# An attention and mixture-of-adapters kernel: products of zeros, the place of one pair's edges, and the piece size of k

## The chip, the cores and the metric

The kernel runs on one core of a Trainium2 chip. The metric is device time in microseconds of one launch: for the kernel before, the median of three runs is 186.81 us (186.53 to 188.19). One more execution was taken with the profiler; its rows are the source of every duration here.

Names of the engines in the rows: PE is TensorE (PEld its weight loads), DVE is VectorE, ACT is ScalarE, POOL is GpSimd, SP is SyncE, which here issues nearly all DMAs. SPq and ACTq are the DMA issues of those two engines.

## The reference

Attention for 8 batches, 8 heads, 576 tokens and head size 64, with a bias that depends on the distance of two tokens alone, and behind it an adapter layer for each token: the two best of 8 experts, each of rank 16.

```python
scores = scale * np.matmul(q, k.transpose(0, 1, 3, 2))
rel = pos[:, None] - pos[None, :]
n = np.abs(rel)                       # buckets of n, all n >= 128 in the last bucket
scores = scores + bias.transpose(2, 0, 1)[None, :, :, :]
attn = np.exp(scores - max); attn = attn / (attn.sum(-1) + 1e-09)
x = np.matmul(attn, v)                # then (B*S, H*D)
...
logits = x @ w_gate                   # top 2 of 8 experts, softmax over the two
delta[mask] += w[mask, k, None] * ((x[mask] @ A[e]) @ B[e])
return x + delta
```

## The kernel before

**Units.** Heads are taken two at a time: a unit u is a batch and a pair of heads, 32 units in all, four to a batch. The 576 tokens of a unit are split into 512 main tokens and the 64 last ones (the "tail"), whose loads and casts are done for a whole batch at a time.

**One unit.** q and k come from memory in float32 into staging tiles (four of each), are cast to bfloat16 (mostly by POOL), and are turned by PE: `turn` (L373) writes the transposes into a score tile in PSUM, and DVE copies them to SBUF. The same turn also takes other items: the tail of a batch (`tl_item`), and blocks of finished outputs on their way to the adapter layer (`x_item`, `zt_item`). Then `keys(u, c)` (L453), four times, forms the scores of 128 keys by 512 queries for both heads (L458), adds the banded part of the bias by products with the table (L463), and ACT takes the exp of the whole 128x1024 tile (L466). `edges(u)` (L507) forms the scores between main and last tokens (L515 and L518, exp in L520). `edge_l` on POOL and `edge_t` on DVE multiply the bias into the edges. `step(u, j)` (L655) multiplies by v and normalises on DVE (L583, L584).

**Score tiles.** Three PSUM tiles of 128x1024 float32 go round in a ring: each turn, each main tile and each edges takes the next one, and waits until the one that had it three places before has been read (by ACT's exp, or by DVE's copies for a turn). Two smaller PSUM tiles serve the products with v and everything else.

**Order.** All of the order is written out by hand: each engine does its instructions in the order in which the program names them, and waits where an input is missing. SP issues loads in program order too. The lines around the change come in this order: the first loads, memsets and the bias table; then products of zeros (`keep_busy`, L677, 128x512 each, whose result nobody reads); the turn of unit 0 together with the tail of two pairs; more zero products; the casts of unit 1's k; edges(0); the turn of unit 1; zero products; DVE's cast of the other tails; `near_first` (L202, one exp of a piece of the bias table Wt on ACT); edges(1); the main tiles of unit 0. Behind the start stands a loop over u from 2: in pass u the unit's main tiles are formed, unit u-1 is multiplied by v, and unit u+2 is turned. `next_edges` (L889) then forms the edges of unit u+1, right behind the transposes, or, where unit u+1 needs the batch tail that this very turn brings (`behind`, L893), after the second half of the step.

**Two ways to load k.** `load` (L102) puts four consecutive tokens of a head on one partition for q, and for k of the units below `WHOLE`: one DMA of 256 KB for the two heads, in pieces of 4 x 64 x 4 bytes = 1 KB. From `WHOLE` on k comes as v does: one DMA of 128 KB for each head, in which the pieces are single tokens, 256 bytes. In the first way the keys lie in another order on the partitions after the turn, so the copy out of the turn takes the four key blocks by themselves with a strided read (L398) and the rest in a second instruction (L400); in the second way one copy (L400) does all. `qk_item` (L411) chooses by naming its closure `keys_done` for the units below `WHOLE`, which `turn` looks at for `n0`.

Of the kernel before, what the change touches and what calls it, by code (L numbers as in the profile page):

```python
# [26 lines left out]
def _ap(t, offset, dims):  # L27

    return bass.AP(tensor=t.tensor, offset=t.offset + offset, ap=[list(t.ap[0])] + dims)
# [8 lines left out]
def kernel(  # L38
# [11 lines left out]
    nc = tc.nc  # L50
# [32 lines left out]
    def score_tile(name, shape=(128, 2, SM), dt=FP32):  # L83
        ring.append(ring.pop(0))
        return scps[ring[-1]].tile(list(shape), dt, name=name, tag="sc")
# [3 lines left out]
    NU = len(units)  # L89


    WHOLE = 4
    NV = 3
    PT = 64 + 2 * SM
    vts = [cp.tile([128, 4, 2, W1], BF16, name=f"v{i}", tag=f"v{i}") for i in range(NV)]
# [6 lines left out]
    def load(u, names="qkv", eng=nc.sync):  # L102
        b, hp = units[u]
        for nm in names:
            src = {"q": q, "k": k, "v": v}[nm]
            t = stg.tile([128, 2, 4 * D], FP32, name=f"{nm}s", tag=f"{nm}s")
            heads = src[b, 2 * hp:2 * hp + 2, :SM, :]
            if nm == "v" or (nm == "k" and u >= WHOLE):
                for h in range(2):
# [91 lines left out]
    def near_first():  # L201
        nc.scalar.activation(Wn[:, 0], Wt[:, 0, NB0:], ACT.Exp, scale=scale)  # L202
# [21 lines left out]
    def table_row(rows, hp, y):  # L224
        return Wn[rows, hp, y - NB0:y - NB0 + 64]

    def turned(h):
        return anti[h * 64:h * 64 + 64, 64 - 64 * h:128 - 64 * h]

    def factors_l(g0, g1):  # L230
        n = (g1 - g0) * 64
        ps = [mp.tile([128, 512], FP32, name="fl", tag="mm") for _ in range(2)]
        for hp in range(g0, g1):
            o = (hp - g0) * 64
            for x in range(2):
                for f in range(2):
                    for h in range(2):
                        nc.tensor.matmul(_ap(ps[h][f * 64:f * 64 + 64], o + x * 16, [[32, 2], [1, 16]]),
                                         lhsT=table_row(slice(h * 64, h * 64 + 64), hp, 256 - 64 * x),
                                         rhs=_ap(turned(h), 2 * f, [[1, 2], [4, 16]]),  # L240
                                         start=(hp == g0 and x == 0), stop=True, skip_group_check=True)
            for h in range(2):
                rows = slice(h * 64, h * 64 + 64)
                nc.tensor.matmul(ps[h][rows, n + o:n + o + 64], lhsT=turned(h),
                                 rhs=table_row(rows, hp, 128), start=False, stop=True, skip_group_check=True)
        for h in range(2):
            rows = slice(h * 64, h * 64 + 64)
            nc.vector.tensor_copy(EL[:, g0:g1, h, :], ps[h][:, :n].rearrange("p (g x) -> p g x", g=g1 - g0))
            nc.vector.tensor_copy(EC[rows, g0 * 64:g1 * 64], ps[h][rows, n:2 * n])
# [120 lines left out]
            t.group, t.k = g, k  # L370
        return g

    def turn(items, copy=nc.vector.tensor_copy, corner=None, after=None, first=None):  # L373
        n = sum(it[1] for it in items)
        n0 = 4 if items[0][0].__name__ == "keys_done" else 0
        assert n <= (16 if corner is None else 12)
        pf = score_tile("tx")
        ps = pf.rearrange("p a x -> p (a x)").bitcast(BF16).rearrange("p (a x) -> p a x", a=2)
        if corner is not None:
            cs = pf[:, :, 384:]  # L380
            corner_scores(corner, lambda hp: cs[:, hp // 2, (hp % 2) * 64:(hp % 2) * 64 + 64],
                          lambda hp: hp % 2 == 0)
        sb = txp.tile([128, 16, 2, 64], BF16, name="tx", tag="tx")
        s0 = 0
        for _, k, src, quarter in items:
            for i in range(k):
                c = s0 + i
                for a in range(2):
                    rows = slice(a * 64, a * 64 + 64)
                    cols = slice(c * 64, c * 64 + 64)  # L390
                    if quarter:
                        for h in range(2):
                            nc.tensor.transpose(ps[h * 64:h * 64 + 64, a, cols], src(i, a, h), ident[rows, rows])
                    else:
                        nc.tensor.transpose(ps[:, a, cols], src(i, a), ident[rows, rows])  # L395
            s0 += k
        if n0:
            (first or copy)(sb[:, :4].rearrange("p c a i -> p (c a i)").rearrange("p (a i c) -> p a i c", a=2, c=4),  # L398
                            ps[:, :, :256].rearrange("p a (c i) -> p a i c", c=4))
        copy(sb[:, n0:n], ps.rearrange("p a (c i) -> p c a i", i=64)[:, n0:n])  # L400
        if after is not None:
            after()
        if corner is not None:
            pxs[corner] = ep.tile([128, HP, 64], BF16, name="pcx", tag="pcx")
            nc.scalar.activation(pxs[corner].rearrange("p (a g) i -> p a (g i)", a=2), cs, ACT.Exp, scale=scale)  # L405
        s0 = 0
        for done, k, *_ in items:
            done(sb, s0)
            s0 += k

    def qk_item(u):  # L411
        n = [nat.pop((u, nm)) for nm in ("k", "q")]

        def done(sb, s0):
            qkT[u] = sb[:, s0:s0 + 8].rearrange("p (n c) a i -> p n (c a i)", n=2)

        def keys_done(sb, s0):
            done(sb, s0)
        return keys_done if u < WHOLE else done, 8, lambda i, a: n[i // 4][a * 64:a * 64 + 64, i % 4].rearrange("p h d -> p (h d)"), False

    def tl_item(b, g0=0, g1=HP):
        n = nat[(b, "qk")]

        def done(sb, s0):
            for hp in range(g0, g1):
                tl[(b, hp)] = sb[:, s0 + hp - g0].rearrange("p a i -> p (a i)")
        return (done, g1 - g0, lambda i, a: n[a * 64:a * 64 + 64, 2 * (g0 + i):2 * (g0 + i) + 2].rearrange(
            "p h d -> p (h d)"), False)
# [24 lines left out]
    def keys(u, c):  # L453
        b, hp = units[u]
        kT, qT = qkT[u][:, 0, :], qkT[u][:, 1, :]
        sc = score_tile("sc")
        for rows, prt, h, f in QUADS:
            nc.tensor.matmul(sc[prt, h, :],  # L458
                             lhsT=kT[rows, c * 128 + f * 64:c * 128 + f * 64 + 64],
                             rhs=qT[rows, :], start=True, stop=False, skip_group_check=True)  # L460
        for rows, prt, h, f in QUADS:
            p0, n, y0 = BAND[2 * c + f]
            nc.tensor.matmul(_ap(sc[prt, h, :], p0, [[128, 4], [1, n]]), lhsT=turned(h),  # L463
                             rhs=band(rows, u, y0, 0, 1, n),
                             start=False, stop=True, skip_group_check=True)
        nc.scalar.activation(probs[u][0][:, c, :, :], sc, ACT.Exp, scale=scale)  # L466
# [20 lines left out]
    def corner_scores(b, place, first):  # L487
        for hp in range(HP):
            t = tl[(b, hp)]
            for h in range(2):  # L490
                rows = slice(h * 64, h * 64 + 64)
                nc.tensor.matmul(place(hp)[rows], lhsT=t[rows, 64:], rhs=t[rows, :64], start=first(hp),
                                 stop=True, skip_group_check=True)
# [13 lines left out]
    def edges(u):  # L507
        b, hp = units[u]
        kT, qT = qkT[u][:, 0, :], qkT[u][:, 1, :]
        t = tl[(b, hp)]  # L510
        sc = score_tile("sc")
        for c in range(4):
            for h in range(2):
                rows = slice(h * 64, h * 64 + 64)
                nc.tensor.matmul(sc[:, h, c * 64:c * 64 + 64], lhsT=kT[rows, c * 128:c * 128 + 128],  # L515
                                 rhs=t[rows, :64], start=(c == 0), stop=True, skip_group_check=True)
        for rows, prt, h, f in QUADS:
            nc.tensor.matmul(sc[prt, h, 256:], lhsT=t[rows, 64:], rhs=qT[rows, f * 256:f * 256 + 256],  # L518
                             start=False, stop=True, skip_group_check=True)
        nc.scalar.activation(probs[u][1][:, 64:], sc.rearrange("p h x -> p (h x)"), ACT.Exp, scale=scale)  # L520
# [156 lines left out]
    def keep_busy(n):  # L677
        for _ in range(n):
            nc.tensor.matmul(busy, lhsT=zero[:, :128], rhs=zero, start=True, stop=True, skip_group_check=True)
# [22 lines left out]
    cast_tail(0, "qk", nc.vector, 0, 2)  # L702
    presets()
    cast(1, "q", nc.gpsimd)
    keep_busy(9)
    turn([qk_item(0), tl_item(0, 0, 2)])
    keep_busy(4)
    for h in range(2):
        cast_half(1, "k", h, nc.vector)
# [1 line left out]
        open_probs(u)  # L711
    edges(0)
    turn([qk_item(1)])
    keep_busy(3)
    cast_tail(0, "qk", nc.vector, 2)
    near_first()
    edges(1)
    keys(0, KO[0])
    cast(2, "q", nc.vector)
    cast(2, "k", nc.gpsimd)  # L720
    keys(0, KO[1])
    factors_l(0, 1)
    edge_l(0)
    keys(0, KO[2])
# [116 lines left out]
    for u in range(2, NU - 2):  # L841
# [40 lines left out]
        items = []  # L882
# [129 lines left out]
    s0 = ring[0]  # L1012
# [109 lines left out]
```

## Time and profile before

| | us |
|---|---|
| median of 3 runs | 186.81 |
| the profiled execution | 187.02 |
| its span, first to last instruction | 185.0 |
| PE busy in the span | 170.3 |
| ACT busy | 163.0 |
| DVE busy | 135.4 |
| POOL busy | 112.4 |

The profiled execution takes 2.0 us more than its span: that lies around the first and the last instruction. PE busy counts a matmul from its start to its modelled end. A row of a timeline gives start, time, engine, line, operation, result and operands, count, and in brackets how long the engine had been idle and what ended that. A row can stand for several instructions that ran together. In rows of DMA issues the time is that of the issue, not of the transfer.

### The profile page before, as it was taken

To read this page: it belongs to the slowest core of one execution; us is meant where nothing else is said; L and a number is where in the kernel's file an instruction comes from. 1 tells how busy PE (TensorE), PEld (TensorE's weight loads), DVE (VectorE), ACT (ScalarE), POOL (GpSimd) and SP (SyncE) were. 2 spreads that over 40 slices of the span, in tenths; PEclk is the share of its full clock that TensorE was granted. 3 is DMA by queue.
4 is the path that set the end of the run, shared out by engine and by line. 5 is a ranking of instruction groups with operands and counts; after the bars stand their busy time and mean duration, and the time that the engine had idled before them with its cause. 6 is when DMAs were issued, how large, how long until landed. Compare 5 with 4: busy or idle time off the path is not lost.

```text
span 185.0 us, 9915 instructions
## 1 busy us (share of the span) xinstructions
PE 170.3 (92%) x4254; PEld 123.4 (67%) x4276; DVE 135.4 (73%) x353; ACT 163.0 (88%) x199; POOL 112.4 (61%) x253
## 2 busy tenths in 40 slices
PE   7988898999998999999999999999999999999980
PEld 2346475776665777777777777777677677788950
DVE  6555875685855787778887798779778888788780
ACT  2189999999897999999999999999999989987880
POOL 8335679357649863985298538955495948435230
PEclk9999999999999999999999999999999999999999
DMA  4899798989889899999979987999988976333337
GB/s 141 214 247 265 179 217 186 235 193 228 212 218 225 200 250 274 233 240 253 244 189 233 262 230 212 227 235 253 246 226 220 267 193 174 121 117 114 117 145 255
DMA packets 93331, 39.26 MB, mean 212 GB/s; under 512 B 78816, under 2 KB 88552, under 8 KB 93288
## 3 DMA queue, kind: packets, MB, share of 16 engines
q1 hardware_dynamic: 92644, 38.16, 79.9%
q8 instruction: 33, 0.54, 1.3%
q10 hardware_dynamic: 644, 0.48, 1.3%
q14 instruction: 10, 0.08, 0.2%
HBM read 29.10 MB, written 9.44 MB: 208 GB/s over the span
## 4 chain that ended last, share of the span: by engine, by line
PE 58%; ACT 10%; DMA 7%; DVE 7%; SPq 5%; issue 5%; POOL 4%; POOLq 0%; DVEq 0%; ACTq 0%
PE pv L544 14%; PE sc L458 11%; ACT pk L466 8%; PE tx L395 6%; PE sc L463 4%; DMA qkt<-in_k_dram 4%; PE sc L515 3%; PE sc L518 3%; PE pv L591 3%; PE pv L561 3%; SPq L110 3%; PE pv L552 3%; DMA vs<-in_v_dram 2%; DMA qs<-in_q_dram 2%; DVE xn L584 2%
## 5 line engine op out<-in xcount | busy, mean ns | idle before, releaser
L466 ACT ACTIVATE pk<-sc 128x1024 bf16<-128x1024 f32 x120 | 113.1, 1032 | 5.1 <-PE sc L463 4.4
L458 PE MATMUL sc<-tx 64*64 64x512 bf16 x480 | 44.3, 389 | 1.8 <-ACT pk L466 0.8
L544 PE MATMUL pv<-v,pk 128*128 128x65 bf16 x992 | 41.3, 193 | 2.8 <-PE sc L463 1.9
L544 PEld LDWEIGHTS <-pk 128*128 128x128 bf16 x1024 | 37.6, 97 | 8.9 <-issue 2.3
L520 ACT ACTIVATE pt<-sc 128x1024 bf16<-128x1024 f32 x32 | 33.5, 1048 | 5.0 <-PE sc L518 4.4
L400 DVE COPY tx<-tx 128x2048 bf16<-128x2048 bf16 (+7 forms) x34 | 33.7, 991 | 2.9 <-PE tx L395 2.6
L463 PE MATMUL sc<-W,anti 64*64 64x192 bf16 (+1 forms) x464 | 34.3, 276 | 0.0
L584 DVE TENSOR_TENSOR xn<-pv,rc 128x320 bf16<-128x320 f32 x62 | 30.5, 491 | 2.1
L583 DVE RECIPROCAL rc<-pv 128x5 f32<-128x5 f32 x62 | 12.0, 193 | 20.6 <-PE pv L591 11.0
L140 POOL CAST kn<-ks 128x512 bf16<-128x512 f32 x30 | 18.7, 623 | 13.5 <-DMA ks<-in_k_dram 8.1
L458 PEld LDWEIGHTS <-tx 64*64 64x64 bf16 x480 | 15.6, 105 | 12.4 <-issue 2.3
L319 DVE TENSOR_TENSOR ot<-dl,xn 128x512 f32<-128x512 f32 x25 | 17.2, 688 | 7.4 <-PE sc L463 5.2
L136 POOL CAST v<-vs 128x512 bf16<-128x512 f32 x32 | 20.4, 636 | 3.3 <-PE pv L563 2.3
L525 POOL TENSOR_TENSOR pt<-pt,EL 128x128 bf16<-128x128 bf16 x32 | 13.7, 427 | 11.4 <-ACT pt L520 8.8
L504 POOL TENSOR_TENSOR pc<-pcx,EC 128x256 bf16<-128x256 bf16 (+2 forms) x9 | 5.6, 619 | 22.8 <-ACT pcx L405 14.2
L140 POOL CAST qn<-qs 128x512 bf16<-128x512 f32 x30 | 18.6, 621 | 0.8 <-DMA qs<-in_q_dram 0.8
L561 PE MATMUL pv<-v,pt 128*128 128x65 bf16 x248 | 17.9, 194 | 0.0
L552 PE MATMUL pv<-vb,pt 128*128 128x130 bf16 x124 | 17.4, 223 | 0.0
L463 PEld LDWEIGHTS <-anti 64*64 64x64 bf16 x480 | 15.1, 107 | 0.2
L561 PEld LDWEIGHTS <-pt 128*128 128x128 bf16 x256 | 14.1, 98 | 0.1
L395 PEld LDWEIGHTS <-kn 64*128 64x128 bf16 x256 | 5.9, 96 | 10.2 <-issue 5.9
L591 PE MATMUL pv<-AW,tx 128*128 128x136 bf16 x124 | 12.5, 224 | 0.0
(149 smaller groups left out, 285.9 us busy)
## 6 DMA issues: line engine op xcount, KB each, us to landing
qs<-in_q_dram SPq DMA_DIRECT2D x32, 256.0 KB, 4.1
vs<-in_v_dram SPq DMA_DIRECT2D x64, 128.0 KB, 4.0
out_dram<-ot SPq DMA_DIRECT2D x32, 256.0 KB, 4.0
ks<-in_k_dram SPq DMA_DIRECT2D x56, 128.0 KB, 4.1
vt<-in_v_dram SPq DMA_DIRECT2D x8, 128.0 KB, 4.5
qkt<-in_q_dram SPq DMA_DIRECT2D x7, 128.0 KB, 4.4
qkt<-in_k_dram SPq DMA_DIRECT2D x7, 128.0 KB, 4.4
out_dram<-ot SPq DMA_DIRECT2D x7, 128.0 KB, 3.1
```

Of the source, the lines that this page charges most:

```text
L136: eng.tensor_copy(t[:, :, :, :D].rearrange("p c h d -> p h c d"), s)
L140: copy(t.rearrange("p c h d -> p h c d"), s)
L400: copy(sb[:, n0:n], ps.rearrange("p a (c i) -> p c a i", i=64)[:, n0:n])
L458: nc.tensor.matmul(sc[prt, h, :], lhsT=kT[rows, c * 128 + f * 64:c * 128 + f * 64 + 64], rhs=qT[rows, :], start=True, stop=False, skip_gro ...
L463: nc.tensor.matmul(_ap(sc[prt, h, :], p0, [[128, 4], [1, n]]), lhsT=turned(h), rhs=band(rows, u, y0, 0, 1, n), start=False, stop=True, ski ...
L466: nc.scalar.activation(probs[u][0][:, c, :, :], sc, ACT.Exp, scale=scale)
L520: nc.scalar.activation(probs[u][1][:, 64:], sc.rearrange("p h x -> p (h x)"), ACT.Exp, scale=scale)
L544: nc.tensor.matmul(pv[:, o:o + W1], lhsT=pk_slice(u, c, h, j + 2 * f), rhs=vm[:, c, h, :], start=first, stop=False, skip_group_check=True)
L552: nc.tensor.matmul(_ap(pv, h * W1, [[130, 2], [1, W1]]), lhsT=probs[u][1][:, x0:x0 + 128], rhs=tvs[b % 2][:, 2 * hp + h].rearrange("p f d ...
L561: nc.tensor.matmul(pv[:, o:o + W1], lhsT=probs[u][1][:, x0:x0 + 128], rhs=vts[u % NV][:, c, h, :], start=False, stop=False, skip_group_che ...
L584: nc.vector.tensor_tensor(xs[b][:, j, hp], _ap(pv, 0, [[W1, 5], [1, D]]), _ap(rc, 6 * j, [[1, 5], [0, D]]), op=ALU.mult)
L591: nc.tensor.matmul(pv[:, o:o + ER + E], lhsT=t.xT[c], rhs=AW[:, c, :], start=first and c == cs[0], stop=(c == HP - 1), skip_group_check=True)
```

## The change

Four edits in three parts.

1. `keep_busy` has ten products ahead of the first turn in place of nine, one zero product between the items inside that turn (`fill=1`), and one in place of three behind the turn of unit 1.
2. `edges(1)` is formed after the first two main tiles of unit 0 in place of before them.
3. `WHOLE` is 10 in place of 4: k of units 4 to 9 comes in one DMA with 1 KB pieces, and their turns copy in two instructions.

```diff
-    WHOLE = 4
+    WHOLE = 10
...
-    def turn(items, copy=nc.vector.tensor_copy, corner=None, after=None, first=None):
+    def turn(items, copy=nc.vector.tensor_copy, corner=None, after=None, first=None, fill=0):
...
         for _, k, src, quarter in items:
+            keep_busy(fill if s0 else 0)
             for i in range(k):
...
-    keep_busy(9)
-    turn([qk_item(0), tl_item(0, 0, 2)])
+    keep_busy(10)
+    turn([qk_item(0), tl_item(0, 0, 2)], fill=1)
     keep_busy(4)
     for h in range(2):
         cast_half(1, "k", h, nc.vector)
...
     turn([qk_item(1)])
-    keep_busy(3)
+    keep_busy(1)
     cast_tail(0, "qk", nc.vector, 2)
     near_first()
-    edges(1)
     keys(0, KO[0])
     cast(2, "q", nc.vector)
     cast(2, "k", nc.gpsimd)
     keys(0, KO[1])
+    edges(1)
     factors_l(0, 1)
```

## The prediction

> **What bounds the kernel now.** I read the page first, then busy time by stage, then the timelines of the engines in the stages where ACT or PE falls short. Columns of the stage rows: stretch and length in us, then busy us (instructions) of PE, PEld, DVE, ACT, POOL, then granted clock, DMA share, GB/s.
>
> ```profile
> span 185.0 us, 9915 instructions
> PE 170.3 (92%) x4254; PEld 123.4 (67%) x4276; DVE 135.4 (73%) x353; ACT 163.0 (88%) x199; POOL 112.4 (61%) x253
> ...
> 45.00:50.00 5.00, 4.67 (x126) 3.47 (x122) 4.49 (x10) 4.34 (x6) 3.88 (x7) 1.00 0.99 233
> 55.00:60.00 5.00, 4.17 (x102) 3.07 (x102) 2.94 (x8) 3.89 (x6) 4.52 (x11) 1.00 0.96 231
> 100.00:160.00 60.00, 58.11 (x1533) 43.29 (x1539) 48.67 (x118) 57.12 (x67) 39.99 (x84) 1.00 0.86 225
> ```
>
> From 100 to 160 us PE is busy 97% and ACT 95%: nothing in the change touches that stretch, and what is won or lost earlier arrives at the end one for one, provided the loads keep up. The room lies before 60 us. From 45 to 50 ACT lacks 0.66 us, from 55 to 60 it lacks 1.11 and PE 0.83, with the DMA engines near full. And the start has gaps of its own.
>
> ```profile
> 1.17 4.02 PE L679 MATMUL busy<-A 128*128 128x512 bf16 x9 [1.17 <-DVE A L166]
> 5.56 0.40 PE L395 MATMUL tx<-ident,kn 64*128 64x64 bf16 x8 [0.37 <-ACT kn L673]
> 6.24 0.29 PE L395 MATMUL tx<-ident,qkb 64*128 64x64 bf16 x4
> 6.46 1.89 PE L679 MATMUL busy<-A 128*128 128x512 bf16 x4
> 8.28 0.39 PE L515 MATMUL sc<-tx 64*128 64x64 bf16 x8
> 9.91 0.78 PE L679 MATMUL busy<-A 128*128 128x512 bf16 x2 [0.34 <-issue]
> 10.62 0.29 PE L515 MATMUL sc<-tx 64*128 64x64 bf16 x8
> 10.97 0.39 PE L458 MATMUL sc<-tx 64*64 64x512 bf16 x4
> 11.19 0.39 PE L463 MATMUL sc<-Wt,anti 64*64 64x192 bf16 x4
> ...
> L679 PE MATMUL busy<-A x15: 380/634/634, 1.2 to 10.3; 128*128 128x512 bf16 x15
> ...
> 9.08 1.02 ACT L520 ACTIVATE pt<-sc 128x1024 bf16<-128x1024 f32 x1 [3.57 <-PE sc L518]
> 10.00 0.35 ACT L202 ACTIVATE Wn<-Wt 128x192 bf16<-128x192 bf16 x1
> 11.19 1.02 ACT L520 ACTIVATE pt<-sc 128x1024 bf16<-128x1024 f32 x1 [0.83 <-PE sc L518]
> 12.11 3.77 ACT L466 ACTIVATE pk<-sc 128x1024 bf16<-128x1024 f32 x4
> ```
>
> From 11.19 us ACT hardly rests, so the start ends when ACT's unbroken run begins. Before it ACT sits idle for PE twice: 3.57 us ahead of pair 0's edges (L520), 0.83 us ahead of pair 1's. The zero products tell the array's speed: 634 ns each at first (median and longest), 380 ns for the last, at 10.3 us. The granted clock reads 1.00 throughout, so the speed of the start has to be read from durations. Edges with their exp take 0.80 us slow (8.28 to 9.08) and 0.57 fast (10.62 to 11.19).
>
> **Part 1: zero products.** The nine start (4.02 - 0.63) / 8 = 0.42 us apart. A tenth goes into the 0.37 us hole before 5.56, where PE waits for the cast kn: it costs nothing. The one between the pair's and the tail's transposes fills the hole before 6.24; slow, it pushes those four back by about 0.2 us, and DVE's copies, which start behind them, too:
>
> ```profile
> 6.57 0.69 DVE L398 COPY tx<-tx 128x512 bf16<-128x512 bf16 x1 [0.39 <-PE tx L395]
> 7.17 0.55 DVE L400 COPY tx<-tx 128x768 bf16<-128x768 bf16 x1
> 5.50 0.61 ACTq L209 DMA_DIRECT2D Wt<-gx  x1
> ```
>
> They end at 7.92 instead of 7.72. What the fillers could buy is the speed: before, two holes of 0.37 and some 0.2 us lie in PE's work just ahead of 6.5 and the array is slow until about 10; without holes it may be fast from about 6.8. Then the four products behind the turn end near 7.5, no longer covering the copies; next late are the copies, and pair 0's edges go at 7.92, their exp at 7.92 + 0.57 = 8.49 in place of 9.08.
> [...]
>
> **Part 2: edges(1) behind the first two main tiles.** Twelve products and one exp move past keys (0, first two), a DVE cast of q2 and a POOL cast of k2; they issue no DMA. Their readers, edge_l(1) and edge_t(1), run after 20 us. Three score tiles go round: the first main tile now takes turn 0's (free at 7.92), the second edges(0)'s (free after its exp), edges(1) the one of turn 1. No order of exps frees one later. With two zero products fewer behind turn 1, keys(0, first) follows that turn's transposes. PE work: edges(0) to about 8.45, sixteen transposes to 8.9, one product to 9.1, the main tile 0.61 us (10.97 to 11.58) to 9.7. ACT: exp of edges(0) 8.49 to 9.41 (0.92 as from 9.08 to 10.00), near_first to 9.77, then the main tile at once. Before, after edges, near_first and edges(1), main tiles began at 12.11; take off the 0.92 of edges(1), which now comes later, and the run starts at 9.77 in place of 11.19: **1.42 us** gained.
> Bounds: the table Wt (its second issue at 5.50) is needed by near_first and by the main tile's bands. It has landed by 10.00, when exactly no row shows; at 10.00 the main tile's exp comes at 10.35 and the gain is 0.84. If the array stays slow, PE is 0.2 late at edges(0) and 0.61 becomes about 1.0: main tile's exp at some 11.0, gain 0.2; if the removed products lie on nothing, a loss of 0.2. I take 1.1, between 0.84 and 1.42.
>
> **Part 3: k in 1 KB pieces for pairs 4 to 9.** Cost of a load, from stretches that move mostly 1 KB pieces (2.6 to 4.2) and 256 B pieces (24.5 to 25.5), and from SP's issues:
>
> ```profile
> 2.60:4.20 1.60, 1.60 (x6) 0.52 (x4) 1.06 (x8) 0.46 (x1) 1.50 (x6) 1.00 1.02 321
> 24.50:25.50 1.00, 1.00 (x37) 0.83 (x29) 0.70 (x2) 1.00 (x2) 0.21 (x1) 1.00 1.11 239
> ...
> 11.81 0.47 SPq L113 DMA_DIRECT2D ks<-in_k_dram  x1
> 15.10 0.97 SPq L110 DMA_DIRECT2D ks<-in_k_dram  x2
> ...
> 42.63 0.62 POOL L140 CAST kn<-ks 128x512 bf16<-128x512 f32 x1 [2.58 <-DMA ks<-in_k_dram]
> 55.25 0.62 POOL L140 CAST kn<-ks 128x512 bf16<-128x512 f32 x1 [1.49 <-PE sc L518]
> 57.30 0.25 POOL L611 TENSOR_TENSOR sm<-a,a 128x32 f32<-128x32 f32 x1
> ...
> 44.42 0.29 PE L395 MATMUL tx<-ident,qkb 64*128 64x64 bf16 x8 [0.27 <-POOL qkb L148]
> 46.92 3.77 ACT L466 ACTIVATE pk<-sc 128x1024 bf16<-128x1024 f32 x4 [0.61 <-PE sc L463]
> 57.58 0.23 ACT L620 ACTIVATE th<-sm 128x32 f32<-128x32 f32 x1 [1.11 <-POOL sm L611]
> ```
>
> A full set of engines moves 321 / 1.02 = 315 and 239 / 1.11 = 215 GB/s: 256 KB takes 0.83 against 1.22 us, 0.39 saved; SP saves 0.50 of issue. SP issues one load after another up to 60 us with hardly a pause, so every later load moves up by 0.4 to 0.5 us per k: about 2 us at k8, over 2.3 at k11. The two late casts of POOL are k8 (2.58 us of waiting) and k11 (1.49; the row names PE, but that matmul is later in the program than this cast, so it can't be what it waits for, and the load of k11 is the other input). POOL's lateness reaches PE as late transposes (44.42) and ACT as 0.61, and as the gate's sum sm (57.30) and 1.11 on ACT. Both waits should vanish even with compute a microsecond earlier. At the first place the whole 0.61 comes back, at the second PE is next late: its 0.83. I take **1.4** (bounds 0 and 1.7).
>
> What this costs: an early pair's turn splits its copy, L398 for the four key blocks (strided), L400 for the rest.
>
> ```profile
> L398 DVE COPY tx<-tx 128x512 bf16<-128x512 bf16 x4 | 2.8, 692 | 2.7 <-PE tx L395 2.7
> L400 DVE COPY tx<-tx 128x512 bf16<-128x512 bf16 x2 | 0.8, 414 | 0.0
> L400 DVE COPY tx<-tx 128x1024 bf16<-128x1024 bf16 x1 | 0.7, 692 | 0.1
> L400 DVE COPY tx<-tx 128x1536 bf16<-128x1536 bf16 x4 | 3.8, 952 | 0.9 <-PE tx L395 0.9
> ...
> 39.84 0.94 DVE L400 COPY tx<-tx 128x1536 bf16<-128x1536 bf16 x1
> 41.17 0.41 PE L458 MATMUL sc<-tx 64*64 64x512 bf16 x4
> ...
> 29.91 0.29 PE L515 MATMUL sc<-tx 64*128 64x64 bf16 x8 [0.17 <-DVE tx L400]
> 30.54 1.02 ACT L520 ACTIVATE pt<-sc 128x1024 bf16<-128x1024 f32 x1 [0.42 <-POOL v L136]
> ```
>
> Eight blocks: 0.692 + 0.414 against 0.692; twelve: 0.692 + 0.692 against 0.952. So 0.42 us more DVE in each of six turns (loop passes 2 to 7), 2.5 us in all. In five of them the copy only frees a score tile for the next pair's second main tile: in pass 5 it ends at 40.78, with 0.42 more at 41.20, and PE takes the tile at 41.17; ACT reads it one exp (0.94) after 41.47. So those are hidden, at 0.03 us of PE; without that cover each costs 0.42. Pass 3 is different: the next pair is the first of batch 1, its edges need the tail columns of this very turn, they wait for the copy (29.91), and ACT is already idle 0.42. There the longer copy costs its whole **0.42**.
>
> **The sum.** Profiled execution 187.02 us (span 185.0 and 2.0 around it), 0.21 over the median of 186.81. 187.02 - 1.1 - 1.4 + 0.42 = 184.94, less 0.21: **184.7 us**.
>
> **Rivals.**
> A (forecast), chance 0.50, 184.1 to 185.4 by the bounds of Wt and of the second gap.
> B: the array stays slow through the start as before. For it: only 0.6 us of holes is closed, and one more product is issued; against it: every PE hole from 1.17 to 8.3 is gone. Gain at the start 0.2 in place of 1.1: 185.6. Chance 0.18.
> C: the change doesn't bring k8 and k11 sooner, since the loads' time lies in other pieces: v stays in 256 B pieces, k10 and later too, and compute that runs a microsecond earlier asks earlier. Then 1.4 goes: 186.1. Chance 0.15.
> D, the slower side: the longer copies. DVE is busy 4.49 of 5 us from 45 to 50; where it comes to a turn's copy more than about 0.9 us late, the copy reaches ACT through the score tile. If all six do, 2.5 us are lost and the gaps of part 3 are only filled by another wait: 187.02 + 2.5 - 1.1 - 0.21 = 188.2, with B's start 189.1. Against it: the other stages have DVE at 60 to 70%. Chance 0.09.
> E: better than forecast, the start at 1.42, both gaps wholly gone (1.7), and pass 3 hidden since its tail k also lands sooner: 187.02 - 3.1 - 0.21 = 183.7 or below. Chance 0.08.
>
> The range from 183.5 to 187.0 leaves out D, and a little of E. One per cent, about what a measurement of this kernel can tell from no change, is 1.87 us: faster is below 184.94, which two thirds of A and E reach, 0.43 with a little of B; slower is above 188.68, D with the slow start and what I haven't seen, 0.07.
>
> **What would show it.** In the changed profile: zero products of 380 ns already among the early ones, exp of edges(0) near 8.5 and of the first main tile near 9.8 with no idle time between; k of pairs 4 to 9 issued by L113; POOL's waits on ks at passes 6 and 8 gone, ACT's 0.61 and 1.11 with them; six L398 more, and a gap of about 0.8 before the edges of pair 4. The prediction is wrong if the first exps come no sooner, if new waits on vs or ks stand where the old ones were, or if ACT waits behind L400 in other passes than 3.

## The result, and the profile after

The changed kernel takes 186.61 us (median of 22 executions), the kernel before 188.2 (22 executions, the three known earlier among them). Ratio 0.9898, 95% interval 0.987 to 0.9927: 1.0% faster, 1.9 us of 188.2, between 1.4 and 2.4. Executions of either kernel scatter by some 3%, so the ratios here compare only those within 1.5% of their kernel's fastest, the medians are of all, and the profiled executions of the change, of a2 and of b1 lie outside that 1.5%. The forecast was 184.7 us, 2.1 below a median of 186.81 that turned out to be a low draw: the size of the gain held, the level that it was taken from did not, and 186.61 is 1.9 above the forecast time.

The profiled execution of the change took 187.19 us, with a span of 185.4: 0.4 more than the one shown of before. As totals the two profiles show no gain; what the change does has to be read from its stages. The start, in the timelines of ACT and PE (lines from 386 on have moved by one: edges are L521, main tiles L467, zero products L680):

```profile
8.40 1.02 ACT L521 ACTIVATE pt<-sc 128x1024 bf16<-128x1024 f32 x1 [2.77 <-PE sc L519]
9.32 0.35 ACT L202 ACTIVATE Wn<-Wt 128x192 bf16<-128x192 bf16 x1
9.61 1.94 ACT L467 ACTIVATE pk<-sc 128x1024 bf16<-128x1024 f32 x2
11.44 1.03 ACT L521 ACTIVATE pt<-sc 128x1024 bf16<-128x1024 f32 x1
...
16.58 0.78 ACT L206 ACTIVATE Wn<-Wt 128x384 bf16<-128x384 bf16 x2 [0.86 <-DMA Wt<-g_d]
17.50 6.58 ACT L467 ACTIVATE pk<-sc 128x1024 bf16<-128x1024 f32 x7
...
6.02 0.39 PE L680 MATMUL busy<-A 128*128 128x512 bf16 x1
6.50 1.04 PE L680 MATMUL busy<-A 128*128 128x512 bf16 x4
7.82 0.29 PE L516 MATMUL sc<-tx 64*128 64x64 bf16 x8 [0.28 <-DVE tx L401]
16.45 0.28 PE L553 MATMUL pv<-vb,pt 128*128 128x130 bf16 x2 [1.20 <-POOL vb L151]
```

The start looks as forecast: the zero product inside the turn takes 390 ns, the four behind it 1.04 us in place of 1.89, edges of pair 0 have their exp at 8.40 (forecast 8.49) and the first main tile at 9.61 (9.77), with no idle time between. But at 16.5 us this execution waits for the table and for the last tokens of v, and the lead is gone: pair 1's main tiles begin at 17.50, before at 17.59:

```profile
17.59 7.71 ACT L466 ACTIVATE pk<-sc 128x1024 bf16<-128x1024 f32 x8
```

Then the stages where the loads had been late, first the waits of POOL and ACT, then busy time by stage with the columns of the prediction's first rows:

```profile
40.75 0.62 POOL L140 CAST kn<-ks 128x512 bf16<-128x512 f32 x1 [0.74 <-DMA ks<-in_k_dram]
53.91 0.62 POOL L140 CAST kn<-ks 128x512 bf16<-128x512 f32 x1
134.58 0.62 POOL L140 CAST kn<-ks 128x512 bf16<-128x512 f32 x1 [1.43 <-DMA ks<-in_k_dram]
...
31.01 1.02 ACT L521 ACTIVATE pt<-sc 128x1024 bf16<-128x1024 f32 x1 [0.75 <-POOL qn L140]
47.13 3.77 ACT L467 ACTIVATE pk<-sc 128x1024 bf16<-128x1024 f32 x4 [0.50 <-PE sc L464]
56.53 0.26 ACT L621 ACTIVATE th<-sm 128x32 f32<-128x32 f32 x1
137.02 0.24 ACT L621 ACTIVATE th<-sm 128x40 f32<-128x40 f32 x1 [0.67 <-POOL sm L612]
```

```profile
45.00:50.00 5.00, 4.71 (x126) 3.44 (x121) 4.03 (x11) 4.50 (x6) 2.44 (x5) 1.00 1.00 231
55.00:60.00 5.00, 4.81 (x138) 3.48 (x135) 3.36 (x10) 4.94 (x7) 4.76 (x13) 1.00 1.04 216
100.00:160.00 60.00, 58.96 (x1505) 42.64 (x1503) 47.74 (x117) 56.14 (x67) 39.50 (x83) 1.00 0.84 219
```

The cast of k8 comes at 40.75 in place of 42.63 and still waits 0.74 us. k11 is no longer waited for in this execution, and with it goes the whole 1.11 us of ACT at the gate (56.53 stands without a wait): from 55 to 60 PE is busy 4.81 us in place of 4.17. In three executions below that come there earlier (b0, a1, b4) POOL still waits 0.81, 1.11 and 0.91 us for k11, and 0.42 to 0.73 of ACT's wait is left. The 0.61 us of ACT ahead of pair 7's main tiles has only become 0.50, so most of it was never k8's: in c1, below, k8's cast waits for nothing (41.53) and ACT's wait is 0.50 all the same. What holds ACT there is not shown. Pair 4's edges wait 0.75 us, the forecast's "about 0.8". New is the last row of ACT: 0.67 us at the gate of pass 24, behind a cast of k27 that waited 1.43 us for its load. From 100 to 160 us ACT does 1.0 us less than before.

So the experiments have three questions: which part carries the 1%, what the start is worth, and where a lead goes on its way to the end. For the last one a compact reading is the time at which ACT begins the exp of a pair's edges (the rows of L520, or of the same line where a file is a few lines longer), from each kernel's timeline of ACT:

| kernel | pair 2 | 3 | 4 | 7 | 10 | 12 | 25 | 26 | 27 |
|---|---|---|---|---|---|---|---|---|---|
| before | 16.02 | 25.20 | 30.54 | 45.28 | 61.33 | 71.05 | 135.63 | 140.49 | 145.35 |
| the change, first profile | 14.69 | 25.34 | 31.01 | 45.58 | 60.48 | 70.20 | 135.29 | 140.78 | 145.69 |
| the change again (b0) | 14.59 | 23.60 | 29.36 | 43.92 | 59.20 | 68.91 | 133.49 | 139.31 | 144.21 |
| loads alone (a1) | 14.85 | 24.03 | 29.70 | 44.27 | 59.85 | 69.56 | 134.19 | 140.06 | 144.97 |
| start alone (a2) | 15.39 | 25.78 | 31.12 | 47.18 | 62.66 | 72.38 | 137.40 | 143.05 | 149.29 |
| products alone (a3) | 14.96 | 24.04 | 29.89 | 45.77 | 61.69 | 71.40 | 135.97 | 142.02 | 146.92 |
| order alone (a4) | 14.67 | 23.90 | 29.24 | 45.05 | 60.97 | 70.68 | 135.32 | 140.63 | 145.54 |
| copies alone (b2) | 14.80 | 24.45 | 30.12 | 44.88 | 60.79 | 70.50 | 135.32 | 140.18 | 145.04 |
| change, not k5 (b4) | 14.55 | 23.72 | 29.06 | 43.62 | 59.00 | 68.71 | 133.42 | 139.63 | 144.53 |
| all k (b3) | 15.02 | 25.47 | 31.14 | 45.70 | 60.60 | 70.32 | 135.21 | 140.07 | 144.93 |
| no products (c1) | 15.84 | 26.85 | 32.52 | 47.08 | 61.98 | 71.70 | 136.32 | 141.19 | 146.04 |
| also every fourth k (c2) | 14.50 | 23.52 | 29.18 | 45.38 | 60.37 | 70.09 | 134.74 | 139.59 | 144.45 |
| early tail of v (b1) | 16.03 | 27.20 | 32.87 | 47.44 | 62.01 | 71.73 | 136.10 | 141.59 | 146.50 |
| c2 without k5 (d1) | 15.09 | 25.15 | 30.49 | 45.05 | 59.95 | 69.67 | 134.33 | 139.26 | 144.12 |

Where nothing is late the steps from pair to pair agree to 0.02 us between kernels (9.71 or 9.72 us from pair 10 to 12 in all fourteen profiles), so a single step shows a single wait.

### The profile page after: what moved, and what is told of

Same layout as the page of the kernel before. It is cut to its first block, busy times and chain, and to the rows that moved or that the text cites. A ratio compares the mean times of both kernels' runs of the same rounds, so it can differ in the third digit from the quotient of the medians.

```text
span 185.4 us, 9934 instructions
## 1 busy us (share of the span) xinstructions
PE 171.7 (93%) x4276; PEld 122.5 (66%) x4276; DVE 136.7 (74%) x359; ACT 163.3 (88%) x199; POOL 113.0 (61%) x253
## 4 chain that ended last, share of the span: by engine, by line
PE 59%; ACT 13%; DMA 8%; POOL 7%; SPq 4%; issue 4%; DVE 3%; POOLq 0%; ACTq 0%; DVEq 0%
PE pv L545 12%; ACT pk L467 11%; PE sc L459 11%; PE tx L396 5%; PE sc L464 4%; PE dl L648 4%; PE sc L516 3%; PE sc L519 3%; DMA qkt<-in_k_dram 3%; PE pv L562 3%; PE pv L553 3%; PE pv L592 3%; DMA vs<-in_v_dram 2%; ACT pt L521 2%; DMA qkt<-in_q_dram 2%
## 5 line engine op out<-in xcount | busy, mean ns | idle before, releaser
L467 ACT ACTIVATE pk<-sc 128x1024 bf16<-128x1024 f32 x120 | 113.3, 1028 | 5.4 <-PE sc L464 4.9
L521 ACT ACTIVATE pt<-sc 128x1024 bf16<-128x1024 f32 x32 | 33.5, 1046 | 3.8 <-PE sc L519 2.8
L401 DVE COPY tx<-tx 128x2048 bf16<-128x2048 bf16 (+7 forms) x34 | 32.0, 942 | 1.2 <-PE tx L396 1.0
```

## The experiments

**The three parts one by one.** a1 is the kernel before with one edit, a2 the changed kernel without it:

```diff
-    WHOLE = 4
+    WHOLE = 10
```

> Part 3 alone: k of pairs 4 to 9 in 1 KB pieces, nothing of the start changed. Theory (the prediction's sum): the two late casts of k cost ACT and PE 1.4 us, the longer copy in pass 3 costs 0.42; so 1.0 us faster, ratio 0.995. Rival 'all from the start': the loads bring nothing and only the copy's cost is left: 0.4 slower, ratio 1.002. Rival 'all from the loads': 1.9 faster, ratio 0.990.

Measured: 186.41 us against 188.62, ratio 0.9842 (0.979 to 0.989).

> Parts 1 and 2 alone: products of zeros and the place of edges(1), k as before. Theory: the first main tile's exp begins near 9.7 us and 1.1 us arrive at the end, ratio 0.994. Rival 'the start's gain is lost on the way', since the table Wt and the last tokens of v land about 16 us whatever the start does: the first exps come as early, but keys of pair 1 begin as late as before (17.5 us), ratio 1.000.

Measured: ratio 0.9895 (0.981 to 0.998), while its median of 189.44 us lies above the 188.62 of before: inconclusive by time. In its profile pair 1's main tiles begin at 17.65 us, as late as the rival said, but for another reason (the step from pair 2 to 3, below).

a3 keeps the new products alone, a4 the new place of edges(1) alone:

```diff
     near_first()
+    edges(1)
     keys(0, KO[0])
...
     keys(0, KO[1])
-    edges(1)
```

> Part 1 alone: only the products of zeros, edges(1) ahead of the main tiles as before. Theory: the array is fast before the edges of pair 0 (zero products of 380 ns from about 6.5 us), their exp near 8.5, edges(1) wait for the copies of turn 1 and their exp begins near 10.5 in place of 11.2: 0.7 us. If the array's speed is what the start lives on, this run has most of a2_start's gain at that place.

Measured: 188.0 us, ratio 1.0035 (0.998 to 1.009).

> Part 2 alone: edges(1) behind two main tiles, products of zeros as before. Theory: the array is slow until about 10 us, three products stand before the main tile, its exp begins near 11.3, and the run of ACT starts 0 to 0.2 us later than before: ratio 1.000. Rival: the order alone is what gains, and the main tile's exp follows near_first at about 10.4: 0.8 us, ratio 0.996.

Measured: 188.26 us, ratio 0.9952 (0.991 to 0.9996).

The loads carry the gain, and more of it than the 0.995 expected (the intervals of a1 and of the whole change still overlap). The products gain nothing that can be measured; the order, half a per cent at the most. The start of a1, which has the old products and the old order, shows why (PE, then ACT):

```profile
3.70 1.03 PE L679 MATMUL busy<-A 128*128 128x512 bf16 x3
5.56 0.29 PE L395 MATMUL tx<-ident,kn 64*128 64x64 bf16 x8 [0.83 <-ACT kn L673]
6.21 0.23 PE L395 MATMUL tx<-ident,qkb 64*128 64x64 bf16 x4 [0.24 <-DVE qkb L148]
6.38 1.04 PE L679 MATMUL busy<-A 128*128 128x512 bf16 x4
...
8.27 1.02 ACT L520 ACTIVATE pt<-sc 128x1024 bf16<-128x1024 f32 x1 [2.77 <-PE sc L518]
9.19 0.35 ACT L202 ACTIVATE Wn<-Wt 128x192 bf16<-128x192 bf16 x1
10.03 1.02 ACT L520 ACTIVATE pt<-sc 128x1024 bf16<-128x1024 f32 x1 [0.48 <-PE sc L518]
```

The array is fast here at 5.6 us, with the old nine products, and it was so ahead of the hole: the last three of the nine take 1.03 us, where three slow ones take 2 x 0.42 + 0.63 = 1.47. The hole of 0.83 us is as long as it is because these products end early. Edges of pair 0 come at 8.27, sooner than in the change (8.40): where the array is fast by then, the product between the transposes costs 0.1 us and buys nothing. In a4 and b2, also with the old products, they come at 8.19 and 8.22. The slow start to 10 us of the first profile of before was that execution's own, not the kernel's.

Whether the fillers help where the array is late is another question, and b0 (the change again, below) bears on it (PE):

```profile
5.83 0.40 PE L396 MATMUL tx<-ident,qn 64*128 64x64 bf16 x8
6.17 0.39 PE L680 MATMUL busy<-A 128*128 128x512 bf16 x1
```

Its transposes at 5.83 are as slow as those of before (0.40 us), and the filler right behind them is fast (0.39); b4 and b1 are much the same (0.39 and 0.43). Before, just as slow there but with holes of 0.37 and about 0.2 us, stayed slow until about 10. That agrees with what the prediction expected of the fillers, but only one execution of the old start was slow at that point, and a3 shows no gain in time.

With a fast array the 0.83 us of idle time ahead of edges(1) is 0.48, and that is the most that the new order can win; at pair 2's edges it is 0.18: 14.67 (a4) in place of 14.85 (a1).

Now the way to the end. The casts of k8 in a2, a3, a4 and b2 (below), whose loads are as before, and in a1:

```profile
44.52 0.62 POOL L140 CAST kn<-ks 128x512 bf16<-128x512 f32 x1 [2.77 <-DMA ks<-in_k_dram]
```
```profile
43.11 0.62 POOL L140 CAST kn<-ks 128x512 bf16<-128x512 f32 x1 [3.21 <-DMA ks<-in_k_dram]
```
```profile
42.39 0.62 POOL L140 CAST kn<-ks 128x512 bf16<-128x512 f32 x1 [3.05 <-DMA ks<-in_k_dram]
```
```profile
42.22 0.61 POOL L140 CAST kn<-ks 128x512 bf16<-128x512 f32 x1 [2.83 <-DMA ks<-in_k_dram]
```
```profile
40.64 0.62 POOL L140 CAST kn<-ks 128x512 bf16<-128x512 f32 x1 [1.93 <-DMA ks<-in_k_dram]
```

In the five profiles with the old loads k8 lands no earlier than 42.2 us (b2), whatever the start does; before has 42.63. a4 is 1.3 us ahead of before at pair 4 and 0.23 at pair 7. The step from pair 6 to 7, 5.07 us in before, is 5.91 in a4 and 6.14 in a3: the earlier start only waits longer there. ACT's wait shows where k8's lateness arrives, from a3: at pair 7's edges, and not at the main tiles behind them, whose wait stays 0.62.

```profile
45.77 1.02 ACT L521 ACTIVATE pt<-sc 128x1024 bf16<-128x1024 f32 x1 [1.10 <-PE sc L519]
```

(In a2, 6.23, all is late, the load of k8 too.) With k of pairs 4 to 7 cheap and k8 itself cheap, k8 is there 1.6 to 2 us sooner, and the same step is 4.9.

**The price of the copies.** b2 is the kernel before with the split copy of part 3 and without its loads:

```diff
-        n0 = 4 if items[0][0].__name__ == "keys_done" else 0
+        n0 = 4 if items[0][0].__name__ in ("keys_done", "keys_split") else 0
...
-        return keys_done if u < WHOLE else done, 8,
+        return keys_done if u < WHOLE else keys_split if u < 10 else done, 8,
```

> The price of part 3 alone: the kernel before, its loads untouched, but the turns of pairs 4 to 9 copy in two instructions as the change does (so the keys of these pairs come out in another order, and meet the bias and values of other keys). Theory: only the turn of pass 3 shows; pair 4's edges come 0.33 to 0.42 us later after pair 3's (5.67 in place of 5.34), nothing else. Rival D: all six turns reach ACT, 2.5 us, ratio 1.013. What is lost at pair 4 may be given back at pass 6, where k8 is late by itself: then the ratio is 1.000.

b4 is the change with pair 5 (turned in pass 3) left as before:

```diff
-            if nm == "v" or (nm == "k" and u >= WHOLE):
+            if nm == "v" or (nm == "k" and (u >= WHOLE or u == 5)):
...
-        return keys_done if u < WHOLE else done, 8,
+        return keys_done if u < WHOLE and u != 5 else done, 8,
```

> The changed kernel, but k of pair 5 loaded in 256 B pieces and copied in one instruction. Theory: the step to pair 4's edges goes back from 5.67 to 5.34 us, every later load comes 0.5 us later than in the change, which no wait up to pair 10 shows; 0.3 us faster than the change at pair 10, at the end 0 to 0.3 since the late loads of pass 24 may take it. Rival: the 0.5 us of SP matter more, and pair 7 or pair 10 wait longer.

Measured: b2 188.8 us against 188.74, ratio 0.9994 (0.994 to 1.005). b4 186.15 us, ratio 0.9885 (0.982 to 0.995). Pair 4's edges in b2, in b4, and the products of these edges in the first profile of the change:

```profile
30.12 1.02 ACT L523 ACTIVATE pt<-sc 128x1024 bf16<-128x1024 f32 x1 [0.75 <-POOL pt L528]
```
```profile
29.06 1.02 ACT L521 ACTIVATE pt<-sc 128x1024 bf16<-128x1024 f32 x1 [0.42 <-POOL sel L853]
```
```profile
30.38 0.29 PE L516 MATMUL sc<-tx 64*128 64x64 bf16 x8 [0.51 <-DVE tx L401]
```

ACT's wait is 0.75 us with the split copy and 0.42 without: 0.33 us, in this pass alone. The rows of ACT name POOL, but PE's products wait for DVE's copy, 0.51 us where before had 0.17. (a3, without split copies, waits 0.94 there; its transposes stand behind a tail load for which POOL waited 2.39 us.) The other five turns show nothing; the steps to pairs 5 and 6 are 4.69 and 4.98 us in b2 as in before, those to 8 and 9 agree to 0.01. So rival D has no support, and the price of part 3 is 0.33 us. At the step to pair 7 none of it is given back (5.09 in b2, 5.07 in before), at pair 10 0.14 (5.78 and 5.92).

**The change again, and all k in 1 KB pieces.**

> The changed kernel once more, beside the next three on one chip. By the first four runs the loads carry the gain (alone 0.984) and the start adds little: ratio 0.985 to 0.990. If the late landing of the last tokens of v and of the table (15.5 and 16.5 us in the first profile of the change) belongs to the change, it is there again, and ACT waits about 0.9 us behind pair 2's edges; if it was that execution's own, the step from pair 2's edges to pair 3's is 9.2 us in place of 10.65.

Measured: 186.72 us against 188.74, ratio 0.9898 (0.985 to 0.994). The late landing at 16.5 us isn't there, pair 3's edges come 9.01 us behind pair 2's, and the span is 183.9. The same kernel thus has a step of 10.65 in one execution and of 9.01 in another, so that landing is not set by the program alone.

The table has more such steps: 10.39 in a2, 10.45 in b3, 10.06 in d1, 11.01 in c1 and 11.17 in b1. They don't have one cause. In d1 POOL and ACT wait for the table, 1.01 and 0.29 us. In a2 and b3 the array itself goes back to half speed. Here are the granted clock of a2 and of b1, from their pages (tenths, in 40 slices of 4.7 us), and four products of a2:

```profile
PEclk9996999999999999999999999999999999999999
PEclk9995899999999999999999999999999999999997
16.75 0.64 PE L459 MATMUL sc<-tx 64*64 64x512 bf16 x4
```

From 15 to 17 us the granted clock is 0.50 in a2 and in b3, and these four products, which take 0.41 us at full speed, take 0.64; ACT then waits 0.58 us for them. Ahead of that PE had stood idle, 1.17 us in a2 and 0.93 in b3 in front of the turn of pair 2, which waits for the cast of k2, and 0.73 behind it: from 11 to 14.4 us it is busy 1.50 and 1.74 us, 2.64 in b0. d1 has such holes too (1.63 us busy) and keeps its speed, so the holes alone don't decide it. The profiles with the old start or half of the new one (before, a1, a3, a4, b2) have steps of 9.08 to 9.65; of the seven with the whole new start four are above 10. Whether the earlier start brings this about, since PE comes to k2 sooner and waits longer for it, is not shown by so few.

```diff
-    WHOLE = 10
+    WHOLE = 32
```

> k of all 32 pairs in 1 KB pieces, otherwise the changed kernel. What is disputed is where the change's lead at pair 12 (0.85 us in the profiles) goes: by pair 27 it is gone. Theory now: the cast of k27, asked for one pass early in pass 24, waits for its load whatever the lead; with all k cheap the wait on ks in pass 24 goes and the steps to pairs 22 and 26 fall to 4.9 us: ratio about 0.980. Rival: DVE, busy 81% there, gets 0.42 us more in every pass of 4.86 and takes more than the loads give: steps above 4.9 everywhere, ratio above 0.99.

Measured: 187.22 us, ratio 0.9944 (0.990 to 0.9986): the time is the rival's, the steps to pairs 22 and 26 (4.86) are the theory's. The change's lead is lost where I looked for it, at the step from pair 25 to 26, 4.86 us in before: the change has 5.49 and 5.82, a1 5.87. The same cast of k27 in before, in b0 and in a1:

```profile
133.93 0.62 POOL L140 CAST kn<-ks 128x512 bf16<-128x512 f32 x1 [0.46 <-DMA ks<-in_k_dram]
```
```profile
133.12 0.61 POOL L140 CAST kn<-ks 128x512 bf16<-128x512 f32 x1 [1.78 <-DMA ks<-in_k_dram]
```
```profile
133.92 0.62 POOL L140 CAST kn<-ks 128x512 bf16<-128x512 f32 x1 [1.87 <-DMA ks<-in_k_dram]
```

b0 arrives 2.1 us ahead at pair 25 and finds k27 0.8 us earlier than before did; a1 arrives 1.4 us ahead and finds it at the same moment. It is not a fixed moment: over the profiles with the old loads of k27 its cast begins between 133.1 and 136.9 us, and b1, which reaches pair 25 later than before does (136.10), still loses 0.6 us at the step to 26. Pass 24 casts two k, and the second is asked for a pass early. In b3 the step is 4.86, so cheap loads of k do remove this wait. But DVE pays in all passes:

```profile
L399 DVE COPY tx<-tx 128x512 bf16<-128x512 bf16 x9 | 6.2, 688 | 0.1
...
80.00:100.00 20.00, 20.00 (x527) 14.15 (x525) 17.43 (x44) 19.26 (x23) 12.98 (x27) 1.00 0.86 235
```

L399 is the added strided copy, nine times from 80 to 120 us, and DVE is busy 17.43 of 20 us, 16.47 in before. Yet the steps show little of it: 0.17 and 0.06 us at pairs 15 and 16, 0.07 at pair 24 and 0.25 at pair 31. By time b3 lies 0.5% behind the change, but the intervals overlap, so that distance is not shown either.

**Only the k that is awaited.**

```diff
+    def whole(u):
+        return u < WHOLE or u % 4 == 3
```

> The changed kernel, with k of pairs 11, 15, 19, 23, 27 and 31 in 1 KB pieces too (each is the second cast of a pass with two). Theory: the lead is lost at the step to pair 26 (5.5 to 6.2 us in four profiles with the change's loads, 4.9 with all k cheap) because k27 lands near 134 us; now the step is 4.9 and k27's cast doesn't wait: 0.6 to 1.0 us faster than the change, ratio 0.985. Rival: six more copies of 0.42 us on DVE at 81% cost as much.

Measured: 186.04 us against 188.95, ratio 0.986 (0.981 to 0.991). The cast of k27 and the gate behind it:

```profile
132.64 0.61 POOL L144 CAST kn<-ks 128x512 bf16<-128x512 f32 x1
```
```profile
135.64 0.27 ACT L625 ACTIVATE th<-sm 128x40 f32<-128x40 f32 x1
```

Neither waits, and the step to pair 26 is 4.85 us: what swallowed the lead is found and taken away, about 1 us in the profile (pair 12 to 27: 74.36 us, b0 75.30). In time c2 can't be told from the change (0.981 to 0.991 against 0.987 to 0.9927). This execution lost 1.6 us at another place: k8 landed at 42.7, as late as with the old loads. It was also issued as late as there, at 37.12 (37.08 in a4, 37.47 in before), so cheap loads don't always move k8 up.

d1 puts b4 and c2 together:

```diff
-        return u < WHOLE or u % 4 == 3
+        return u != 5 and (u < WHOLE or u % 4 == 3)
```

> The two findings together: k of pairs 4 to 9 except 5, and of 11, 15, 19, 23, 27 and 31, in 1 KB pieces; the start as in the change. Theory: the step to pair 4's edges is 5.34 us (5.67 in the change) and the step to pair 26 is 4.9 (5.5 to 6.2), so 0.3 and 0.6 to 1.0 us less than the change: ratio 0.984 against the kernel before. Rival: 0.5 us of issue more for k5 makes k8 late at pass 6, and the step to pair 7 is above 5.1 again.

Measured: 185.99 us against 188.44, ratio 0.9886 (0.985 to 0.993). Steps to pairs 4, 7 and 26: 5.34, 4.89 and 4.93, all as expected. The ratio isn't: 0.984 lies just outside the interval. By time d1 is faster than the kernel before and not shown faster than the change.

**The start once more.** c1 leaves out all zero products, b1 moves loads of the start:

```diff
-    keep_busy(10)
-    turn([qk_item(0), tl_item(0, 0, 2)], fill=1)
-    keep_busy(4)
+    turn([qk_item(0), tl_item(0, 0, 2)], fill=0)
...
-    keep_busy(1)
```

> The changed kernel with no product of zeros at all. In every profile but the first one of the kernel before, the array is fast by 6.5 us, with the old products as with the new. [...]

Measured: 185.92 us, ratio 0.9835 (0.978 to 0.989). The array stays slow (PE):

```profile
7.86 0.40 PE L516 MATMUL sc<-tx 64*128 64x64 bf16 x8 [1.25 <-DVE tx L401]
...
10.85 0.43 PE L519 MATMUL sc<-tx 64*64 64x256 bf16 x4
...
17.80 0.69 PE L459 MATMUL sc<-tx 64*64 64x512 bf16 x4
...
20.07 0.41 PE L459 MATMUL sc<-tx 64*64 64x512 bf16 x4
```

430 ns at 10.85 us, where the change has 300, and still slow at 17.80, 0.69 us for four products that take 0.41 at 20.07: the speed comes near 20 us. Pair 2's edges come at 15.84, 1.15 us behind the first profile of the change; the time at the end is no worse than the change's (ratio 0.9835 and 0.9898). So it is with the products, nine as well as ten, that the array is fast early (by 6.7 us, by 10.3 in the first profile of before), and that speed is worth nothing that can be measured at the end.

```diff
         table_first(h, nc.scalar)
+    load_tail(0, "v", eng=nc.scalar)
...
-    load(0, "v")
-    load_tail(0, "v")
     for h in range(2):
         table(h)
+    load(0, "v")
```

> The changed kernel, with the last tokens of v (batch 0) issued by ACT near 6.2 us in place of SP at 9.3, and the two loads of the bias table ahead of v of pair 0. In three of ten profiles so far pair 3's edges come 10.4 us or more behind pair 2's in place of 9.2, with DVE or ACT waiting for the last tokens of v or the table. Theory: that wait goes, the step is 9.2 or less every time, and the median falls by 0.3 to 0.5. Rival: the loads of v of pair 0, now later, or ACT's 0.6 us of issue ahead of the first exp take as much.

Measured: 188.31 us, ratio 0.9928 (0.985 to 1.001); the theory missed. k2 and v of pair 0 come later instead:

```profile
12.21 0.62 POOL L140 CAST kn<-ks 128x512 bf16<-128x512 f32 x1 [4.84 <-DMA ks<-in_k_dram]
...
15.79 0.62 POOL L136 CAST v<-vs 128x512 bf16<-128x512 f32 x1 [2.58 <-DMA vs<-in_v_dram]
```

The step to pair 3 is 11.17 us, the longest of all, but not by the loads alone: PE waited for k2, and from 14 to 19 us the granted clock is 0.50 (the second PEclk row above). The DMA engines are full in this stretch (share 1.09 from 8 to 12 us, 1.01 in the change), so an earlier load is probably paid for by its neighbours; one profile doesn't show more.

## Why the prediction was right in its sum and wrong in its parts

Time, direction and size held: 186.61 us lies in the range, near its upper end of 187.0, since the kernel before is slower than its first three runs said; 1.0% was measured where 1.1% was forecast. The step that failed is in part 1: "before, two holes of 0.37 and some 0.2 us lie in PE's work just ahead of 6.5 and the array is slow until about 10". I read it from one execution and took it for the kernel's. a1, a4 and b2 have the old products and are fast by about 5 us; their edges of pair 0 come at 8.19 to 8.27, sooner than the 8.49 forecast for the change. The first profile of before had simply drawn a late change of speed: the same products took 634 ns there in the median and 390 in a1. I had made of that speed a chance for rival B, an estimate of mine, instead of asking what the kernel before does in its other executions. The rest of that step, that without holes a slow array may be fast from about 6.8, was an estimate too: no run of the kernel before shows the 6.8 on which the 8.49 and the start's term rest. What the runs showed in its place doesn't refute it: b0, b4 and b1 are slow at 5.8 us and fast by 6.7, and pair 0's edges come at 8.40 in the first profile of the change and at 8.55 in b0. (The 634 and 380 ns stand in a ratio of 1.67; the distance of the starts, 0.42 us slow and (1.04 - 0.38) / 3 = 0.22 fast, is nearer to two.)

So the **start's term of 1.1 us** was mis-sized. Against the profiled execution of before it is 1.33 at pair 2 (16.02 to 14.69). Against a kernel before with a fast array (14.80 in b2, 14.85 in a1) it is 0.1 to 0.35 in the change's two profiles, b4 and c2 (14.50 to 14.69), and a loss of 0.2 to 0.6 in b3, d1 and a2 (15.02 to 15.39), which cast k2 at 11.55 to 11.85 us in place of 11.03 to 11.35. What is won comes from the new order (14.67 in a4, 14.96 in a3); with the old loads even that is lost at k8.

The **loads' term of 1.4 us** held where it was worked out. k8 is there about 2 us sooner (42.2 to 43.1 with comparable starts, 40.4 to 40.8 now where it is waited for, c2 excepted). From pair 4 to pair 12 the kernels with the old loads (before, a2, a3, a4, b2) take 40.4 to 41.5 us, the change 39.2 and 39.6, a1 39.9; between the two first profiles it is 40.51 to 39.19, or 1.32. It came from other places than I named, though. "POOL's lateness reaches PE as late transposes (44.42) and ACT as 0.61" had the place wrong: k8's lateness arrives at pair 7's edges, 0.17 us in before (5.07 to 4.90), and the 0.61 behind them only became 0.50, worth 0.09 at the step to pair 8. The other 1.06 came at pair 10 in place of the 0.83, and in executions that come there earlier less of it: 0.69 in b0, 0.38 in a1. By time the loads alone bring more than 1.4 less the copy: 0.9842 of 188.6 is 3.0 us, with an interval from 2.0 to 3.9. Part of it may be that a kernel which comes to pass 6 earlier waited longer there (0.8 to 1.1 us in a3 and a4), and the profiled execution of before (187.02 us) is one of its faster ones (median 188.2), so it can't show all that a usual one loses; the rest no profile shows, and it stays open.

The **cost of 0.42 us** in pass 3 was 0.33, and alone in being seen, as forecast. What was said against rival D, that DVE is at 60 to 70% in the other stages, misread the rows: DVE is busy 3.82 of the 4 us from 20 to 24 and 3.46 of those from 36 to 40. The copies stay hidden there all the same.

"Arrives at the end one for one, provided the loads keep up" needed its proviso: they don't at pass 24. That is what rival C said of later pieces, at another place; of the 2.1 and 1.5 us by which the change (b0) and a1 are ahead of before at pair 12, 1.0 and 1.1 are lost by pair 27, at k27.

So the sum came out right with one term nearly missing and another larger than forecast, which is luck in part.

## What to carry to other kernels

A load whose landing is set by the stream of loads, and not by the compute that waits for it, is a gate: what is won ahead of it is lost there (at k8 a4's lead of 1.3 us became 0.23), and a profile shows only the rest of the wait. Before summing gains of several places, find the gates between them and the end, and ask of each what it does with an earlier arrival. And a state that an execution draws (here the array's speed in the first 10 us) is not a property of the kernel, and needs a second profile before a term of the sum rests on it. Look also at what an engine that comes earlier then waits for: here PE stood idle for k2, and in two of seven profiles with the new start it lost its speed behind that hole (granted clock 0.50).

## What the runs showed of the hardware

- The same nine products of zeros left the array fast (380 to 390 ns for one, 634 slow) by about 5 us in a1, a4 and b2 and by 10.3 in before; with the ten, and one more between the transposes, it was fast by 6.7 us in all nine profiles; without any it was still slow at 17.80 us (0.69 us for four products, 0.41 at 20.07). The granted clock read 1.00 in all of these slow stretches.
- The array went back to half speed with holes of no more than 1.17 us in PE's work: in a2 and b3 PE was busy 1.50 and 1.74 us from 11 to 14.4, and from 15 to 17 us the granted clock was 0.50. d1, busy 1.63, kept its speed.
- Two loads of 120 KB from memory written by the kernel itself (the table), at the same place of the same program, took 6.1 us in the median to land in the first profile of the change and 4.6 in b0; pair 3's edges came 10.65 and 9.01 us behind pair 2's.
- One SP issue in every 4 to 6 us takes 1 to 2.9 us in place of about 0.5 (2.86 in a1, 2.39 in b0), with 1 KB pieces as with 256 B pieces (in the change 1.05 for a q at 38.88, 2.33 for two of v at 40.54). What holds it was not tried.
